# x, weights and result laid out by partitions, a finer fill of the head, turns in transposing mode and maxima through DRAM in a fused GFNet and gated feed-forward kernel

## The chip, the cores and the metric

The kernel runs on one core of a Trainium2 chip. The metric is the device time of that core in microseconds (us). Before the change the median of three runs is 418.23 us (418.14 to 418.61).

The engines are called by the profile's names: PE (TensorE, matrix products), PEld (loading of its weights), DVE (VectorE), ACT (ScalarE), POOL (GpSimd) and SP (SyncE, which here issues DMAs).

## The reference, cut to what matters

x has 2048 rows of 512 values; F is 1376.

```python
xn = _layernorm(x)                                   # over the last axis
s = irfft2(rfft2(xn, axes=(-2, -1)) * (w_r + 1j * w_i), s=(S, D), axes=(-2, -1))
gate, up = xn @ W_gate, xn @ W_up                    # 512 -> 1376
h = relu(gate) * up
return x + s * silu(h @ W_down)                      # 1376 -> 512
```

## The kernel before

Everything that PE multiplies is split into two numbers of 16 bits, a high and a low part, and each product is made in three passes (high by high, high by low, low by high). Scales keep the parts in range: for each block of 128 columns of the weights a power of two from the sum of their squares, for the down weights and for the Fourier filter one from a maximum over the whole matrix.

The 2048 rows of x are worked on in eight chunks of 256. A chunk is two "rows" of 128 partitions. The rows of x go over the partitions so that the first stage of the Fourier transform is a product with a 64 x 64 matrix. Feed-forward works on pairs of chunks, four blocks of 512 columns (the text calls them chunks 0 to 3 of the feed-forward, as the tiles' names do: `gu0_...` to `gu3_...`).

**The head.** x of chunks 0 and 1 and the gate and up weights (groups 0 to 6 of `GROUPS`, line 22; groups 0, 1 and 2 have one block of 128 columns, the others two) are loaded. `stats` (310) makes means and variances on DVE, `deviation` (321) their inverse roots (with a root `q` on ACT), `normalise` (365) `xf`. `turn_row` (399) turns one row of 128 by four products in 32 bits with a unit matrix from the constants `cS`; ACT copies the high part from PSUM into `xT`, DVE subtracts the low one. For the weights, ACT squares each block with a sum over the row (`squares`, 489, an `ACTIVATE` with two results, `wgu` and `m`, and a read of the accumulator), PE adds the partitions by a product with ones (`group_scale`, 499), DVE makes the scale `p`, then a high part `wgu<-raw,p` is made on ACT where `HIGH_ACT` says so (else on DVE) and a low part on DVE (`group_split`, 507). Twelve times three products of ones that nobody reads (`keep_busy`, 391, tile `idle`) run on PE first. The first three gate and up pairs are made in two halves of 256 columns (`product`, from 1033), all later ones on 512.

**The rest.** `product` makes a gate or up block `gu` of twelve products of 512 columns; ACT rectifies the gate block (`r`), DVE multiplies (`h32`), and high and low parts `h16` are made. `down` makes a group of three products `dn`. Between these PE runs the Fourier transform: eight first stages `s1` (`first_stage`, 24 products on 64 x 64 pieces each), whose split results `t1` go to DRAM (`A_d`); eight middle chunks (`fft_chunk`: `at` is loaded from `A_d`; on PE `y`, `xx`, `z` and `v`; between them DVE makes `a16`, `xsp`, the products `tt` with the filter, `pf`, `p16`, `z16` and `t9`), which store to `C_d`; eight last stages `s2` (`last_stage`, PE again in 64 x 64 pieces); and `finish` (976), which multiplies by the gate, adds x and stores. The down weights' maximum (`down_scale`) and the filter's (`filter_scale`) are made by `greatest` (551): a product that turns a column into a row, a maximum on DVE, and a product of ones that spreads it.

**What sets the order.** Nothing of this is issued in the order of the code. Each operation is a `step` (100) with an engine, a cost in us, what it reads and writes and perhaps a due time. `run` (119) works due times back through the dependencies and simulates the engines: at each point, of the steps of an engine that could begin within 0.06 us of the earliest, it takes the one that is due first. The order that comes out is the program's order on each engine, and each engine keeps it. Steps with a `mode` are products in small pieces (1 for the Fourier stages `s1`, `s2`, 2 for `y`, 3 for the last up product); the planner charges `MODE` us when PE changes between modes (182). The due times of the stages come from the table in lines 33 to 41 (`FIRST` and `FIRST_STEP` for the first stages, `MID` for the middle, `LAST` for the last ones, `DOWN` for the down weights), `tick` (668) gives those of the feed-forward. On chip, semaphores order what depends on each other. Most records of the profile have line 64, since the helper `InOrder` (56) issues every instruction; what an instruction is must be read from its tiles.

Of the kernel before, what the change touches and what calls it, by code (L numbers as in the profile page):

```python
# [230 lines left out]
def kernel(ctx: ExitStack, tc: tile.TileContext, x, wg, wu, wd, wl, ew, sp, c_r, c_d, c_m, c_x, c_s, out):  # L231
    nc = tc.nc
    PS = bass.MemoryType.PSUM
    xr, outr = (t[0].rearrange("(p e n) d -> e p n d", p=N1, n=NE) for t in (x, out))
# [33 lines left out]
    DVE.memset(ones, 1.0)  # L268
    warm = cpool.tile([P, 1], F32, name="warm")
# [22 lines left out]
    def load_x(c):  # L292
        tile_of(f"x{c}", "k4", [P, 2, D], F32)
        for e in range(2):
            engine, queue = (("SP", SP), ("ACT", ACT))[c == 0 and e]
            for i in range(2) if c == 0 else [None]:
                rows = slice(2 * c, 2 * c + 2) if i is None else slice(i, i + 1)
                to = slice(0, 2) if i is None else slice(i, i + 1)
                step(engine, .6, lambda e=e, queue=queue, rows=rows, to=to: queue.dma_start(T[f"x{c}"][64 * e:64 * e + 64, to], xr[e, :, rows, :]),
                     writes=[(f"x{c}", e, i)], lead=14 if c else None, kb=256 if i is None else 128, lag=2.2, due=(LOADX[c] + (i or 0) * .01) if c < 2 else None)  # L300
# [302 lines left out]
    def filter_scale(due):  # L603
# [323 lines left out]
    def last_stage(c, due):  # L927
# [24 lines left out]
        def put(e, op, to, a, b, n, reads, write, port=True):  # L952
            eng, cost = ((DVE, dve(n)), (POOL, pool(n)))[e == "POOL"]
# [228 lines left out]
```

## Time and profile before

| | before |
| --- | --- |
| runs, median | 418.23 us |
| the profiled execution | 417.77 us |
| its span | 416.0 us |
| PE busy | 404.9 us (97%) |
| DVE busy | 307.2 us (74%) |
| ACT busy | 188.4 us (45%) |
| POOL busy | 45.7 us (11%) |

The profile is one execution. Its span goes from the first to the last record, its own time is some 1.8 us longer. Times in the rows are from the span's start. An engine at 97% over the span can still be idle where it matters: the span's first 16 us and its last 5 are read apart from the rest. A row of the timeline gives start, length, engine, line, operation, what it writes `<-` what it reads, the shape and in brackets the idle time ahead of it and what ended that; a run of like instructions is one row with a count.

### The profile page before, as it was taken

How to read it: one execution, taken by the hardware profiler on the slowest of the kernel's cores; microseconds unless marked ns; L12 is line 12 of the kernel's file. 1: busy time of each engine (PE TensorE's matmuls, PEld its weight loads, DVE VectorE, ACT ScalarE, POOL GpSimd, SP SyncE). 2: the span in 40 equal slices, each digit the busy share in tenths (PEclk: the TensorE clock that was granted, in tenths of full speed). 3: DMA queues.
4: the chain of work that ended last, by engine and by line, in shares of the span. 5: the costliest groups of instructions: out<-in, count | busy, mean ns of one | idle time of the engine just before them, and what ended most of it. 6: DMA issues, size and time to landing. Idle time of an engine off the chain costs nothing.

```text
span 416.0 us, 7674 instructions
## 1 busy us (share of the span) xinstructions
PE 404.9 (97%) x2997; PEld 214.8 (52%) x2997; DVE 307.2 (74%) x648; ACT 188.4 (45%) x356; POOL 45.7 (11%) x68
## 2 busy tenths in 40 slices
PE   7799999999999999999999999999999999899995
PEld 5686454544444444545555456456455445444554
DVE  3748999999998898335585977897763427899943
ACT  3769863545444259420344335435414336432311
POOL 0000000000000000001130321330330018301300
PEclk9699999999999999999999999999999999999999
DMA  8992211055424787963005145053402189575614
GB/s 204 337 337 60 67 36 50 2 151 55 98 52 100 163 249 221 246 222 116 0 2 166 28 138 165 3 165 84 135 2 52 50 205 212 143 203 137 166 54 101
DMA packets 41764, 51.72 MB, mean 124 GB/s; under 512 B 16064, under 2 KB 24864, under 8 KB 41728
## 3 DMA queue, kind: packets, MB, share of 16 engines
q1 hardware_dynamic: 40880, 50.59, 45.6%
q10 hardware_dynamic: 848, 0.66, 0.6%
q8 instruction: 23, 0.38, 0.4%
q14 instruction: 13, 0.11, 0.1%
HBM read 35.48 MB, written 12.60 MB: 116 GB/s over the span
## 4 chain that ended last, share of the span: by engine, by line
PE 91%; DMA 5%; DVE 1%; ACT 1%; issue 0%; ACTq 0%; SPq 0%; DVEq 0%
PE gu L64 51%; PE dn L64 27%; PE z L64 3%; PE xx L64 3%; PE s L64 2%; DMA xt<-in_x 2%; DMA ct<-C_d 2%; PE y L64 2%; PE v L64 2%; DMA raw<-in_wu 1%; PE head L64 1%; PE dn_3b L64 1%; DVE xT L64 0%; DVE ye L64 0%; ACT xT L64 0%
## 5 line engine op out<-in xcount | busy, mean ns | idle before, releaser
L64 PE MATMUL gu<-xT,wgu 128*128 128x512 f16 (+1 forms) x1032 | 216.0, 367 | 3.4 <-ACT r L64 1.2
L64 PEld LDWEIGHTS <-wgu 128*128 128x128 f16 x1032 | 100.6, 99 | 108.4 <-issue 6.7
L64 PE MATMUL dn<-wds,h 128*128 128x512 f16 (+2 forms) x528 | 115.5, 372 | 0.0
L64 PEld LDWEIGHTS <-h 128*128 128x128 f16 (+1 forms) x561 | 53.7, 98 | 58.3 <-issue 2.5
L64 ACT ACTIVATE h<-h 128x512 f16<-128x512 f32 (+1 forms) x44 | 27.7, 629 | 70.2 <-DVE h L64 70.1
L64 DVE TENSOR_TENSOR h<-gu,r 128x512 f32<-128x512 f32 (+2 forms) x52 | 33.6, 646 | 22.6 <-PE gu L64 21.4
L64 POOL TENSOR_TENSOR po<-tt,tt 128x256 f32<-128x256 f32 x16 | 14.8, 926 | 285.1 <-DVE tt L64 236.8
L64 ACT ACTIVATE r<-gu 128x512 f32<-128x512 f32 (+1 forms) x44 | 26.0, 592 | 20.6 <-PE gu L64 20.3
L64 DVE TENSOR_TENSOR h<-h,h 128x512 f16<-128x512 f32 (+1 forms) x44 | 30.0, 690 | 4.5 <-ACT h L64 4.2
L64 POOL TENSOR_TENSOR ae<-zz 128x128 f32<-128x128 f32 (+1 forms) x32 | 19.3, 636 | 60.9 <-ACT zz L64 47.6
L64 DVE SCALAR_TENSOR_TENSOR tt<-xsp,cw,wt 128x512 f32<-128x512 f32 x32 | 25.2, 849 | 0.0
L64 ACT ACTIVATE g<-dn,cdi 128x512 f32<-128x512 f32 (+1 forms) x16 | 10.6, 673 | 25.1 <-PE dn L64 25.1
L64 DVE TENSOR_TENSOR z<-z,z 128x1024 f16<-128x1024 f32 x8 | 9.8, 1222 | 15.4 <-ACT z L64 15.4
L64 DVE TENSOR_TENSOR sv<-sv,g 128x512 f32<-128x512 f32 (+1 forms) x17 | 10.8, 671 | 9.6 <-ACT g L64 8.9
L64 DVE BATCH_NORM_STATS2 st<-x 128x6 f32<-128x512 f32 x16 | 10.9, 683 | 9.3 <-DMA x<-in_x 9.3
L64 PE MATMUL gu<-xT,wgt 128*64 128x256 f16 (+1 forms) x144 | 17.0, 309 | 0.0
L64 DVE TENSOR_TENSOR a<-y,a 128x1024 f16<-128x1024 f32 x8 | 9.7, 1218 | 8.3 <-ACT a L64 8.3
L64 ACT ACTIVATE wgu<-raw 128x512 f16<-128x512 f32 x20 | 12.4, 622 | 6.5 <-DMA raw<-in_wu 6.4
L64 DVE SCALAR_TENSOR_TENSOR wgu<-raw,p,wgu 128x512 f16<-128x512 f32 x20 | 14.5, 746 | 0.5 <-ACT wgu L64 0.4
L64 DVE TENSOR_TENSOR xt<-xt,sv 128x512 f32<-128x512 f32 (+1 forms) x17 | 11.5, 693 | 4.1 <-DMA xt<-in_x 4.1
L64 ACT ACTIVATE xs<-xs 128x1024 f16<-128x1024 f32 x8 | 8.5, 1058 | 12.6 <-DVE xs L64 12.6
L64 PEld LDWEIGHTS <-wgt 128*64 128x64 f16 (+1 forms) x144 | 9.6, 106 | 7.1 <-issue 1.7
(135 smaller groups left out, 432.5 us busy)
## 6 DMA issues: line engine op xcount, KB each, us to landing
A_d<-t SPq DMA_DIRECT2D x16, 256.0 KB, 3.2
rw<-in_wl SPq DMA_DIRECT2D x8, 512.0 KB, 6.5
wt<-in_wl SPq DMA_DIRECT2D x8, 512.0 KB, 4.7
at<-A_d SPq DMA_DIRECT2D x8, 512.0 KB, 4.6
C_d<-t SPq DMA_DIRECT2D x16, 256.0 KB, 3.3
ct<-C_d SPq DMA_DIRECT2D x16, 256.0 KB, 6.1
xt<-in_x SPq DMA_DIRECT2D x32, 128.0 KB, 3.0
out<-xt SPq DMA_DIRECT2D x30, 128.0 KB, 2.3
```

What stands on the lines that cost most here:

```text
L64: return lambda *args, **kw: self.tc.keep_in_program_order(f(*args, **kw))
```

## The change

1. **Layouts.** x, the result and the gate and up weights are put in DRAM by the host so that each partition's data lie together (for the weights group by group). A load of x is one DMA over 128 partitions in place of two over 64, a load of weights has one piece per partition in place of four, `finish` loads and stores once over 128 partitions. No load stands on ACT's queue any more: all are on SP's.
2. **The fill.** `keep_busy` issues 67 single products of ones in place of 36 in triples, as steps without due times, which the planner puts wherever PE would be waiting. They go to the upper half of a tile `small`, whose lower half takes the sums of the first two groups (so both have no `sum` tiles of their own).
3. **The turns.** The first chunks' rows are turned with PE's transposing operation; the unit matrix is made on POOL, and `cS` shrinks from 135 columns to 7.
4. **The maxima.** `greatest` stores the column to DRAM, loads it back spread over all partitions as rows, and reduces on DVE. The two products are gone.
5. **Joining.** Where PE has just run a step with a mode, the planner looks for steps with mode 1 or 2 that could begin and are due within `JOIN` (18.81 us) and prefers the same mode.
6. **Tables.** New due times; for the chunks 0 and 1 the first row of `xf` is made on ACT; other high parts on ACT; copies and sums of the last stage get a margin of 0.4 us in the plan.

```diff
-T0, DOWN, FIRST, FIRST_STEP, MID, MID_STEP, LAST, LAST_STEP = 10.0, 56.9, 49.0, 16.8, 180.6, 14.5, 265.2, 14.8
+T0, DOWN, FIRST, FIRST_STEP, MID, MID_STEP, LAST, LAST_STEP = 7.1, 57.9, 51.9, 17.1, 155.2, 14.9, 307.4, 10.8
...
-NORM, TURN1 = (('DVE', 'DVE'), ('DVE', 'ACT')), 'PE'
+NORM, TURN1 = (('ACT', 'DVE'), ('ACT', 'DVE')), 'PE'
...
-                    t, s = min((k for k in at if k[0] <= soon), key=lambda k: (k[1].due, k[1].order))
+                    now = [k for k in at if k[0] <= soon]
+                    if e == "PE" and mode:
+                        now = [k for k in now if 0 < k[1].mode < 3 and k[1].due < k[0] + JOIN] or now
+                    t, s = min(now, key=lambda k: (e == "PE" and k[1].mode != mode if mode else 0, k[1].due, k[1].order))
...
+    POOL.memset(unit, 0.0)
+    POOL.affine_select(out=unit, in_=unit, compare_op=ALU.not_equal, fill=1.0, base=0, pattern=[[-1, P]], channel_multiplier=1)
...
+        for i in range(1 + (c == 0)):
+            rows = slice(i, i + 1) if c == 0 else slice(0, 2)
+            step("SP", .5, lambda rows=rows: SP.dma_start(T[f"x{c}"][:, rows], x[:, 2 * c + rows.start:2 * c + rows.stop, :]),
...
-            step("PE", .43, lambda: [matmul(T["idle"], w[:, 0:P], w, start=True, stop=True) for _ in range(3)],
-                 writes=["idle"], due=1. + .43 * k, lead=0.)
+            step("PE", .213 if k < 26 else .11, lambda: matmul(T["small"][:, 256:], w[:, 0:P], w, start=True, stop=True), writes=[("small", "idle")])
...
-                matmul(head()[:, cols], T[f"xf{c}"][:, i, cols], cS[:, 7:], start=True, stop=True)
-        step("PE", 1., run, reads=[(f"xf{c}", i), "cS"], writes=[(f"head{c}", i)])
+                PE.transpose(head()[:, cols], T[f"xf{c}"][:, i, cols], unit)
+        step("PE", .45, run, reads=[(f"xf{c}", i)], writes=[(f"head{c}", i)])
...
-        step("PE", .31, lambda: matmul(T[f"row_{name}"][0:1, :], col, cS[:, 7:], start=True, stop=True),
-             reads=["cS", *reads], writes=[f"row_{name}"], due=due, margin=MARGIN)
-        step("DVE", .25, lambda: DVE.tensor_reduce(top[0:1, :], T[f"row_{name}"][0:1, :], axis=AX.X, op=ALU.max),
-             reads=[f"row_{name}"], writes=[f"max_{name}"])
-        step("PE", .31, lambda: matmul(T[f"all_{name}"], ones[0:1, :], top[0:1, :], start=True, stop=True),
-             reads=[f"max_{name}"], writes=[f"all_{name}"], due=due + 2, margin=MARGIN)
+        step("SP", .6, lambda: SP.dma_start(row.rearrange("a p -> p a"), col), reads=reads, writes=[f"row_{name}"], due=due, kb=8)
+        step("SP", .6, lambda: SP.dma_start(rows, row.broadcast_to([P, P])), reads=[f"row_{name}"], writes=[f"rows_{name}"], kb=64)
+        step("DVE", .22, lambda: DVE.tensor_reduce(top, rows, axis=AX.X, op=ALU.max), reads=[f"rows_{name}"], writes=[f"all_{name}"], due=due + 6)
...
+            step("SP", .5, lambda t=t, cols=cols: SP.dma_start(out[:, 2 * c + i, cols], t()), reads=[(n, part)], kb=w // 2, due=due, lag=2.2)
```

What the planner makes of it on the engines, at the places that the prediction speaks of. First ACT in the head, before (`wgu,m<-raw` is a square with its sum, `wgu<-raw,p` a high part, `xT<-head` the copy of a turned row; the digit behind `wgu` and `raw` is the group):

```order
L64 DMA x0_115<-in_x 64x512 x2
L64 DMA raw0_1_126<-in_wu 128x4x128
L64 ACTIVATE wgu0_76,m0_173<-raw0_1_126 128x512
L64 ACTIVATE q0_171<-q0_171 128x2
L64 ACTIVATE wgu0_76,m0_173<-raw0_0_131 128x512
L64 ACTIVATE wgu1_77,m1_186<-raw1_0_139 128x512
L64 ACTIVATE wgu1_77,m1_186<-raw1_1_144 128x512
L64 ACTIVATE wgu0_76<-raw0_0_131,p0_201 128x512
L64 ACTIVATE xT0_214<-head0_196 128x512 x2
L64 ACTIVATE wgu0_76<-raw0_1_126,p0_201 128x512
```

And ACT at the same place with the change:

```order
L64 ACTIVATE q0_172<-q0_172 128x2
L64 ACTIVATE wgu0_77,m0_193<-raw0_0_133 128x512
L64 ACTIVATE xf0_196<-x0_121,q0_172 128x512
L64 ACTIVATE wgu0_77,m0_193<-raw0_1_137 128x512
L64 ACTIVATE xT0_222<-head0_208 128x512 x2
L64 ACTIVATE wgu1_78,m1_240<-raw1_0_141 128x512
L64 ACTIVATE wgu0_77<-raw0_0_133,p0_233 128x512
L64 ACTIVATE wgu1_78,m1_240<-raw1_1_146 128x512
L64 ACTIVATE wgu2_79,m2_260<-raw2_0_154 128x512
L64 ACTIVATE wgu2_79,m2_260<-raw2_1_158 128x512
```

ACT's two kinds of DMA issue are gone, a row of `xf` is new on it, and the two `xT` copies stand behind three rows in place of five squares and high parts. Behind the rows shown come the root for chunk 1, two high parts of group 1, three squares of group 3, a high part of group 2, chunk 1's row of `xf`, one more square and the two `xT` copies of chunk 1. On PE the order is now 44 products of the fill, four transposes (the row of `xf` from DVE), two of the fill, four transposes (the row from ACT), two of the fill, the sum of group 0, 19 of the fill, the sum of group 1 and the first product; before it was 36 of the fill, the sum of group 0, eight products with the unit matrix, the sum of group 1 and the first product. SP's queue begins with x of chunk 0 (two DMAs), x of chunk 1 and then the weights group by group; before it began with `cS`, half of x of chunk 0, weights, and x of chunk 1 only behind group 1.

Then SP's queue where the Fourier transform's middle begins, before (`t1` to `A_d` is the store of a first stage, `at` the load for a middle chunk, `DMA_TRANSPOSE` a turn of x for the feed-forward's last chunk):

```order
L64 DMA_TRANSPOSE xT3_1866<-x16_6_1652 128x16x128
L64 DMA_TRANSPOSE xT3_1866<-x16_7_1671 128x16x128
L64 DMA cX_74<-in_c_x 64x256
L64 DMA cD_73<-in_c_d 128x2048
L64 DMA cm0_1971<-in_c_m 128x512
L64 DMA A_d_69<-t1_7_1965 128x1x1024 x2
L64 DMA wt_0_1988<-in_wl 128x1024
L64 DMA at_0_2027<-A_d_69 128x2x1024
L64 DMA wt_0_1988<-E_d_71 2x2x128
L64 DMA at_1_2136<-A_d_69 128x2x1024
```

And with the change (`rows_mw` is the filter's maximum, loaded back):

```order
L64 DMA rows_mw_111<-row_mw_110 128x128
L64 DMA E_d_71<-edge2_114 64x2x16
L64 DMA wt_0_1791<-E_d_71 2x2x128
L64 DMA A_d_69<-t1_6_1892 128x1x1024 x2
L64 DMA A_d_69<-t1_7_1910 128x1x1024 x2
L64 DMA cm1_1957<-in_c_m 128x512
L64 DMA_TRANSPOSE xT3_1975<-x16_6_1690 128x16x128
L64 DMA at_0_1988<-A_d_69 128x2x1024
L64 DMA at_1_1992<-A_d_69 128x2x1024
```

One turn now stands between the last store to `A_d` and the first load from it, the other behind both loads. Before, both stood ahead of the store.

Last, DVE where the middle's first chunks pass, before:

```order
L64 TENSOR_TENSOR z16_0_2408<-z0_2366,z16_0_2408 128x1024
L64 TENSOR_TENSOR xsp_1_2427<-xx1_2395,xo1_2425 128x256
L64 TENSOR_TENSOR xsp_1_2427<-xx1_2395,xo1_2425 128x4x32
L64 TENSOR_TENSOR xsp_1_2427<-xo1_2425,xx1_2395 128x4x32
L64 SCALAR_TENSOR_TENSOR tt0_1_2433<-xsp_1_2427,cw_87,wt_1_2194 128x512
L64 SCALAR_TENSOR_TENSOR tt1_1_2448<-xsp_1_2427,cw_87,wt_1_2194 128x512
L64 SCALAR_TENSOR_TENSOR tt2_1_2452<-xsp_1_2427,cw_87,wt_1_2194 128x512
L64 SCALAR_TENSOR_TENSOR tt3_1_2454<-xsp_1_2427,cw_87,wt_1_2194 128x512
L64 TENSOR_TENSOR h32_2_1_2475<-gu2_1_1_2435,r2_1_2450 128x512
L64 TENSOR_TENSOR pf_1_2526<-po_1_2456 128x4x32 x4
L64 TENSOR_TENSOR t9_0_2528<-v0_2458,t9_0_2528 128x2x512
L64 TENSOR_TENSOR a16_2_2547<-y2_2477,a16_2_2547 128x2x8x64
```

And with the change:

```order
L64 TENSOR_TENSOR a16_2_2404<-y2_2346,a16_2_2404 128x2x8x64
L64 TENSOR_TENSOR pf_1_2328<-po_1_2308 128x4x32 x4
L64 TENSOR_TENSOR p16_1_2451<-pf_1_2328,p16_1_2451 128x1024
L64 TENSOR_TENSOR z16_0_2459<-z0_2426,z16_0_2459 128x1024
L64 TENSOR_TENSOR xsp_2_2481<-xx2_2462,xo2_2479 128x256
L64 TENSOR_TENSOR xsp_2_2481<-xx2_2462,xo2_2479 128x4x32
L64 TENSOR_TENSOR xsp_2_2481<-xo2_2479,xx2_2462 128x4x32
L64 SCALAR_TENSOR_TENSOR tt0_2_2514<-xsp_2_2481,cw_88,wt_2_2254 128x512
L64 SCALAR_TENSOR_TENSOR tt1_2_2516<-xsp_2_2481,cw_88,wt_2_2254 128x512
L64 SCALAR_TENSOR_TENSOR tt2_2_2536<-xsp_2_2481,cw_88,wt_2_2254 128x512
L64 SCALAR_TENSOR_TENSOR tt3_2_2541<-xsp_2_2481,cw_88,wt_2_2254 128x512
L64 TENSOR_TENSOR z16_1_2534<-z1_2489,z16_1_2534 128x1024
```

Chunk 1's filter products are now made before `z16` of chunk 0, and those of chunk 2 come between `z16` of chunk 0 and that of chunk 1; with them the chunks stand closer together. The middle begins ahead of the last up product of the feed-forward's chunk 1 and its down groups; before it began behind that product and the down groups of two of the four rows.

The joining shows on PE. Before, two pairs of the sixteen `s` stages stood together (`s2` of chunks 1 and 2, and of 3 and 4). Now seven do: `s1` of chunks 0 and 1, 4 and 5, 6 and 7, and `s2` of 0 and 1, 2 and 3, 4 and 5, 6 and 7; `y` of chunks 0 and 1 is one block too. Runs of products in small pieces, each entered from large products, are 23 in place of 27. The last pair of `s2` now stands behind the last up product of the feed-forward's chunk 3; before, `s2` of chunk 7 stood just ahead of it.

More of the change, by code (lines that the diff above doesn't have):

```diff
@@ L293, in load_x @@
         tile_of(f"x{c}", "k4", [P, 2, D], F32)
[L294 to L300, printed above, removed]
+        for i in range(1 + (c == 0)):
+            rows = slice(i, i + 1) if c == 0 else slice(0, 2)
+            step("SP", .5, lambda rows=rows: SP.dma_start(T[f"x{c}"][:, rows], x[:, 2 * c + rows.start:2 * c + rows.stop, :]),
+                 writes=[(f"x{c}", i)], lead=14 if c else None, kb=256 * (rows.stop - rows.start), lag=2.2, due=(LOADX[c] + i * .01) if c < 2 else None)
     def x_names(c, i):
-        return [(f"x{c}", e, None if c else i) for e in range(2)]
+        return [(f"x{c}", 0 if c else i)]
     def stats(c, q, j):
@@ L481, in load_group @@
         w = sum(fwidth(f) for f in GROUPS[g])
-        f0 = GROUPS[g][0] * P
         for i, src in enumerate((wg, wu)):
-            tile_of(f"raw{g}_{i}", "k4", [P, 4, 2 * P], F32)
-            e, queue = (("SP", SP), ("ACT", ACT))[g == 0 and i]
-            step(e, .6, lambda i=i, src=src, queue=queue: queue.dma_start(T[f"raw{g}_{i}"][:, :, :w], src.rearrange("(k p) f -> p k f", p=P)[:, :, f0:f0 + w]),
+            tile_of(f"raw{g}_{i}", "k4", [P, 4, w], F32)
+            of = src[:, 4 * P * GROUPS[g][0]:4 * (P * GROUPS[g][0] + w)].rearrange("p (k f) -> p k f", k=4)
+            step("SP", .5, lambda i=i, of=of: SP.dma_start(T[f"raw{g}_{i}"], of),
                  writes=[f"raw{g}_{i}"], lead=12 if g else None, kb=2 * w, lag=2.5, due=LOADS[g])
@@ L500, in group_scale @@
         nf = len(GROUPS[g])
-        tile_of(f"sum{g}", "dn" if g < 2 else "F", [P, 4], F32)
+        if g > 1:
+            tile_of(f"sum{g}", "F", [P, 4], F32)
+        to, name = ((lambda: T[f"sum{g}"]), f"sum{g}") if g > 1 else ((lambda: T["small"][:, 4 * g:4 * g + 4]), ("small", g))
         tile_of(f"p{g}", "p", [P, 2, 4], F32)
-        step("PE", .2, lambda: matmul(T[f"sum{g}"][:, :2 * nf], ones, T[f"m{g}"][:, :2 * nf], start=True, stop=True),
-             reads=[(f"m{g}", j, i) for j in range(nf) for i in range(2)], writes=[f"sum{g}"])
-        step("DVE", .52, lambda: scale_of(T[f"sum{g}"][:, :2 * nf], T[f"p{g}"][:, :, :2 * nf], 9), reads=[f"sum{g}"], writes=[f"p{g}"], port=True)
+        step("PE", .2, lambda: matmul(to()[:, :2 * nf], ones, T[f"m{g}"][:, :2 * nf], start=True, stop=True),
+             reads=[(f"m{g}", j, i) for j in range(nf) for i in range(2)], writes=[name])
+        step("DVE", .52, lambda: scale_of(to()[:, :2 * nf], T[f"p{g}"][:, :, :2 * nf], 9), reads=[name], writes=[f"p{g}"], port=True)
     def group_split(g):
@@ L585, in run @@
             b = p.bitcast(I32)
-            DVE.tensor_scalar(p[:, 0:1], T["all_md"], 1e-30, 1e30, op0=ALU.max, op1=ALU.min)
+            DVE.tensor_scalar(p[:, 0:1], all_md, 1e-30, 1e30, op0=ALU.max, op1=ALU.min)
             DVE.tensor_scalar(b[:, 0:1], b[:, 0:1], 0x7F800000, None, op0=ALU.bitwise_and)
@@ L952, in put @@
         def put(e, op, to, a, b, n, reads, write, port=True):
-            eng, cost = ((DVE, dve(n)), (POOL, pool(n)))[e == "POOL"]
-            step(e, cost, lambda: getattr(eng, op)(to(), a(), b()), reads=reads, writes=[write], port=port)
+            eng, cost = ((DVE, dve(n)), (POOL, pool(n) + .2))[e == "POOL"]
+            step(e, cost, lambda: getattr(eng, op)(to(), a(), b()), reads=reads, writes=[write], port=port, margin=LATE)
         def copy(to, of, reads, write):
-            step("ACT", .11, lambda: ACT.activation(to(), of(), AF.Copy), reads=reads, writes=[write])
+            step("ACT", .11, lambda: ACT.activation(to(), of(), AF.Copy), reads=reads, writes=[write], margin=LATE)
         copy(lambda: ac()[:, :, 64:65], lambda: a0()[:, :, 64:65], [zn], (aen, 4))
@@ L986, in finish @@
             step("DVE", dve(w), lambda s=s, t=t: DVE.tensor_add(t(), t(), s()), port=True,
-                 reads=[(sn, 3 + i, part), (n, "x", 0), (n, "x", 1)], writes=[(n, part)])
-            for e in range(2):
-                engine, queue = (("SP", SP), ("ACT", ACT))[e and c == NCH - 1 and i]
-                step(engine, .6, lambda t=t, cols=cols, e=e, queue=queue: queue.dma_start(outr[e, :, 2 * c + i, cols], t()[64 * e:64 * e + 64]),
-                     reads=[(n, part)], kb=w // 4, due=due, lag=2.2)
+                 reads=[(sn, 3 + i, part), (n, "x")], writes=[(n, part)])
+            step("SP", .5, lambda t=t, cols=cols: SP.dma_start(out[:, 2 * c + i, cols], t()), reads=[(n, part)], kb=w // 2, due=due, lag=2.2)
     step("SP", .6, lambda: SP.dma_start(cR, c_r), writes=["cR"], lead=20, kb=256)
-    step("SP", .6, lambda: SP.dma_start(cS, c_s), writes=["cS"], kb=70, due=LOADU)
+    step("SP", .6, lambda: SP.dma_start(cS, c_s), writes=["cS"], kb=4, lead=20)
     step("SP", .6, lambda: SP.dma_start(cD, c_d), writes=["cD"], lead=20, kb=512)
     step("SP", .6, lambda: SP.dma_start(cX, c_x), writes=["cX"], lead=20, kb=128)
+    tile_of("small", "dn", [P, D], F32)
     keep_busy(BUSY)
@@ L1180 @@
     r = run_bass_kernel_spmd(nc, [arrays], core_ids=[0])
-    return r.results[0]["out_0"]
+    return np.asarray(r.results[0]["out_0"]).reshape(2, N1, NE, D).transpose(1, 0, 2, 3).reshape(1, S, D)
```

45 lines of the change are left out of this document (23 added, 22 removed).

## The prediction, made before the changed kernel ran

> **What bounds the kernel now.** I read the page's chain first, then the waits of TensorE (PE), then the head stage by stage. The page says how much of the span PE works, and which work ended last:
>
> ```profile
> PE 404.9 (97%) x2997; PEld 214.8 (52%) x2997; DVE 307.2 (74%) x648; ACT 188.4 (45%) x356; POOL 45.7 (11%) x68
> PE 91%; DMA 5%; DVE 1%; ACT 1%; issue 0%; ACTq 0%; SPq 0%; DVEq 0%
> ```
>
> The answer on who waited for whom has few rows for PE, here the two longest (us in total, times, longest):
>
> ```profile
> PE sum L64 <- ACT wgu L64: 1.5, 1, 1.5
> PE gu L64 <- ACT r L64: 1.2, 1, 1.2
> ```
>
> The first lies in the head, ahead of the first product, as do the shorter ones left out; the second is far behind. So the time is that of PE's own stream, plus what comes before the first product, plus the tail. A change pays in three ways only: the products start earlier, PE's stream gets shorter, or a wait of PE goes. The head cut into windows (PE's busy us and count, then PEld, DVE, ACT, POOL, PE clock, DMA share, GB/s):
>
> ```profile
> 0.00:3.45 3.45, 2.40 (x12) 1.71 (x13) 0.19 (x2) 1.49 (x2) 0.20 (x4) 1.00 0.34 95
> 3.45:6.87 3.42, 3.42 (x18) 2.42 (x17) 0.97 (x3) 0.00 (x0) 0.00 (x0) 1.00 0.97 245
> 6.87:10.28 3.41, 1.50 (x13) 1.06 (x11) 2.26 (x9) 2.14 (x7) 0.00 (x0) 0.99 1.12 271
> 10.28:13.70 3.42, 3.42 (x16) 3.42 (x17) 1.46 (x5) 1.35 (x4) 0.00 (x0) 0.51 1.15 266
> 13.70:17.11 3.41, 1.30 (x12) 0.98 (x12) 2.93 (x9) 3.16 (x8) 0.00 (x0) 0.99 1.08 359
> 17.11:20.52 3.41, 3.41 (x19) 2.43 (x17) 3.27 (x12) 3.13 (x9) 0.00 (x0) 0.51 1.05 381
> ```
>
> A window in which PE was busy for 1.50 or 1.30 us is followed by one at half clock (0.51). The second of these holds products: it costs 1.7 us.
>
> **The head.** These rows carry it, in order of time (start, duration):
>
> ```profile
> 4.58 0.69 DVE L64 BATCH_NORM_STATS2 st<-x 128x6 f32<-128x512 f32 x1 [3.56 <-DMA x<-in_x]
> 6.78 0.69 DVE L64 BATCH_NORM_STATS2 st<-x 128x6 f32<-128x512 f32 x1 [1.28 <-DMA x<-in_x]
> ...
> 8.74 0.61 ACT L64 ACTIVATE wgu<-raw 128x512 f16<-128x512 f32 x1
> 9.26 0.19 ACT L64 ACTIVATION_READ_ACCUMULATOR wgu<-raw 128x1 f32 x1
> ...
> 10.25 3.66 PE L64 MATMUL head<-cS,xf 128*128 128x128 f32 x16 [0.37 <-DVE xf L64]
> ...
> 16.40 5.65 PE L64 MATMUL gu<-xT,wgu 128*128 128x256 f16 x35 [1.05 <-DVE xT L64]
> ...
> 23.34 1.95 PE L64 MATMUL head<-cS,xf 128*128 128x128 f32 x16
> 25.12 8.22 PE L64 MATMUL gu<-xT,wgu 128*128 128x256 f16 x72
> ```
>
> Products run from 16.40; at 25.12 plus 24 of them (8.22/72 = 0.114 each), so at 27.8, the first three gate and up pairs are done for half the rows. From there PE's only wait is the 1.2 for r. I ask when the changed kernel gets to that point.
>
> Its loads stand on one queue: x of chunks 0 and 1 (1.05 MB), then the first weights (0.26 MB). By the windows' rates 1.17 MB have moved by 6.87 and the rest at 271 GB/s by 7.4; x, now alone in front, lands near 4.2 and 4.8 instead of 4.58 and 6.78 (estimate: the first DMA leaves 0.4 earlier and shares with nothing). So the statistics end near 6.1, and **ScalarE (ACT) becomes the pace setter**. Its durations, by form:
>
> ```profile
> L64 ACT ACTIVATE wgu<-raw,p 128x512 f16<-128x512 f32 x11 | 7.6, 716 | 0.2
> L64 ACT ACTIVATE xT<-head 128x512 f16<-128x512 f32 x4 | 2.3, 596 | 5.1 <-PE head L64 5.0
> L64 ACT ACTIVATE xf<-x,q 128x512 f32<-128x512 f32 x1 | 0.8, 816 | 0.1
> ```
>
> A square with its read takes 0.71 (8.74 to 9.45). In the new order from 7.4: square 8.1, xf 8.9, square 9.6, two xT 10.8, square 11.5, high part 12.3, square 13.0; PE's sum for the second group stands ahead of the first product, so that starts near 13.2 (16.40 before). Behind it: two squares, q (0.2), two high parts, three squares, a high part, xf: 19.7. PE's four products (12 x 0.114 = 1.4 each) are done by 18.8, so it waits 0.9 for these rows of x. The eight transposes have no row. With the old form sixteen passes take 25.12 - 23.34 = 1.8; sixteen at half a 256-column product are 0.9, eight 0.5; below that nothing, since they must stream. I take 0.6, nearest the eight. Then two products: 23.0. **Gain 4.8.** If only PE's work bound it (18.8 + 0.6 + 2.7 = 22.1), 5.7; with one half-clock window left among the products, 3.1. The early copies that this needs are covered by DVE's and ACT's idle time; without that cover the gain falls to the 3.2 of the earlier start alone.
>
> The fill: 44 unread products stand ahead of the first transpose. As before, 30 of them (12 + 18 in the first two windows) run by 6.87, and the other 14, at 0.114, last to about 8.5; the first row of xf is ready at 7.9, the second at 8.9. So the fill costs the first transposes 0.6, which the 13.2 does not feel: ACT's two squares and the high part end later than its xT copies anyway. The identity made on GpSimd (POOL) has no row; it has 7 us to be ready, beside nothing on that engine. I take nothing, at most 1.
>
> **The maxima.** Where a product of one row breaks into the stream:
>
> ```profile
> 36.08 18.29 PE L64 MATMUL gu<-xT,wgu 128*128 128x512 f16 x84
> 54.21 0.28 PE L64 MATMUL sum<-m,ones 128*128 128x4 f32 x2
> ...
> 60.52 5.35 PE L64 MATMUL gu<-xT,wgu 128*128 128x512 f16 x24
> 65.81 0.38 PE L64 MATMUL row_md<-cS,md 128*1 128x128 f32 x2
> 66.12 2.76 PE L64 MATMUL gu<-xT,wgu 128*128 128x512 f16 x12
> ```
>
> 84 products take 18.13, 0.216 each. So 24 from 60.52 end at 65.70, and the next begins at 66.12: 0.42, four times: **1.7 gained**. In their place come two DMAs, one behind the other, for each maximum. A like round trip is that of A_d:
>
> ```profile
> 169.25 0.85 PE L64 MATMUL s<-xs,cR 64*64 64x257 f16 x24
> ...
> 173.09 1.19 SPq L64 DMA_DIRECT2D A_d<-t  x2
> ...
> 178.25 0.39 SPq L64 DMA_DIRECT2D at<-A_d  x1
> ...
> 182.34 0.20 DVE L64 COPY am<-at 128x126 f16<-128x126 f16 x1 [3.04 <-DMA at<-A_d]
> ```
>
> From the store's issue to the loaded data that is 9.2 for 0.5 MB each way; 8 KB and 64 KB should take less, and not less than half: 4.6 to 9.2, I take 6. On SP the loads of x for chunks 2 and 3 queue behind it; DVE reads them thirteen rows after the reduction that waits for the same trip, so I cost that at nothing. On VectorE (DVE) the reduction stands twelve rows behind md's (five of 0.75, two of 0.69, smaller ones, about 6 in sum), so DVE stands still for 0 to 3. PE has four products of 2.6, two first stages and five more before the first down product, 21 in all, against about 15 until the first weights are split (their low part stands behind t of stage 0 on DVE, which is later than the trip). Cost 0.
>
> **Joined stages.** Single and paired last stages before:
>
> ```profile
> 339.40 0.85 PE L64 MATMUL s<-ct,cR 64*64 64x257 f16 x24
> 340.19 2.76 PE L64 MATMUL gu<-xT,wgu 128*128 128x512 f16 x12
> 342.88 1.51 PE L64 MATMUL s<-ct,cR 64*64 64x257 f16 x48
> 344.33 2.76 PE L64 MATMUL gu<-xT,wgu 128*128 128x512 f16 x12
> 347.02 1.51 PE L64 MATMUL s<-ct,cR 64*64 64x257 f16 x48
> 348.47 5.35 PE L64 MATMUL gu<-xT,wgu 128*128 128x512 f16 x24
> ```
>
> Twelve products take 2.59, so the entry at 342.88 costs 0.10; a stage alone takes 0.79 + 0.10, a pair 1.45 + 0.10: 0.23 for each pair. The order has 7 pairs of s against 2, and y of chunks 0 and 1 in one: 6 x 0.23, less 2 lost neighbourhoods of unlike stages at 0.1: **1.2 gained**. The wait of 1.2 for r came behind five stages within 9.1 us (339.40 to 348.47), all of which ACT copies out; now they come in twos with four products between: **1.2 gained** (0 if another takes its place).
>
> **The FFT's middle** starts earlier in PE's row, ahead of chunk 1's last up product and its down groups. Before, its first data came 13.1 after the last forward stage (169.25 to 182.34). Now the order gives PE 17 us of work from stage 6 to the first y (the pair, five products, four down groups of 0.65). The data needs 13.1, 0.7 for the second stage, and on SP a transposing DMA now stands ahead of the load of at (min, median, max ns):
>
> ```profile
> L64 SPq DMA_TRANSPOSE xT<-x x6: 1738/2766/6637, 99.1 to 168.9; - x6
> ```
>
> If its issue (1.7 to 6.6, median 2.8) fell wholly behind the store, y could begin after 15.5 to 20.4, 16.6 by the median: ready by about the time PE comes. A little later DVE is the tighter one:
>
> ```profile
> L64 DVE SCALAR_TENSOR_TENSOR tt<-xsp,cw,wt 128x512 f32<-128x512 f32 x32 | 25.2, 849 | 0.0
> L64 DVE TENSOR_TENSOR z<-z,z 128x1024 f16<-128x1024 f32 x8 | 9.8, 1222 | 15.4 <-ACT z L64 15.4
> ```
>
> From the start of z_1 on PE to v_1 there are z_1 (1.3), v_0 (0.8), and five down groups of 0.65: 5.4. DVE has z_0 (1.2), three xsp (1.0), four tt (3.4), z_1 (1.2): 6.8, some 0.5 less where they overlap: v_1 waits about 0.9. **I take 1.2 lost** in this stretch, 0 to 4 as bounds.
>
> **The tail** after the last product (411.2) is one chain of copy, two DVE rows and a store. It stays, with one store of 128 partitions for two of 64:
>
> ```profile
> 408.43 2.79 PE L64 MATMUL dn_3b<-wds,h 128*128 128x256 f16 x24
> ```
>
> I take 0.1 lost. Halved issues on SP and the last stage's new margins touch no engine that PE waits for; nothing.
>
> **Sum**, against the profiled execution's 417.77 (span 416.0; the median of the runs is 418.23, 0.1% more): 4.8 + 1.7 + 1.2 + 1.2 - 1.2 - 0.1 = 7.6, so **410.2**.
>
> **Rivals.** *More from the head, nothing lost later*: ACT's squares arrive in better rhythm, PE's work alone binds (5.7), the middle loses nothing: 408.1. For it: DMA ran at 359 to 381 later in the head. *The clock still falls*, the change doing less than it says: the fill stops before xf, and the transposes leave a window as thin as 1.50; one half-clock window among the products costs 1.7: 411.9. For it: only 0.2 of fill stands between the transposes. The trace shows nothing of transposing mode. The Trainium skill, "TensorE: Matmul & The Clock Gate", Part 4, says that full clock "doesn't engage for transpose-mode (it doesn't count as PE-busy the same way)", which would favour this rival; no run here shows it yet, and by it the time would be 411.9. *The middle eats the gain*: at 4 lost there and a new wait for r, 414.2. *Slower*: the same mechanism in full. Every chunk's z and v wait for DVE, which is at 74% and gets its eight chunks closer together; 16 such waits pass the 8.8 gained elsewhere from 0.55 each on, and at 0.7 each the time is 420.2. Against it: of those sums only v_1's came out short.
>
> **How the numbers follow.** Forecast 410.2, chance 0.52; more head 0.15; clock 0.11; middle 0.13; slower 0.05; the rest (0.04) unchanged, gains and losses cancelling. The lower bound is all gains at their best, 417.77 - 5.7 - 1.7 - 1.4 - 1.2 = 407.8, less 0.8 for loads that land earlier: 407. The upper takes the small head (3.1) and 3.4 lost in the middle with the r wait kept: 417.77 - 3.1 - 1.7 - 1.2 + 3.4 = 415.2. A measurement of this kernel tells about 0.2% from no change.
>
> **What would show it.** First product near 13.2, the third pair's end near 23.0; granted clock 0.99 in every window from 6.87; no row_ or all_ product; gaps of 0.10 at four fewer entries; no wait of PE for r; a wait before v_1 of about 1. Wrong it would be by a clock of 0.5 after the transposes, by PE waits for DVE spread over the middle, or by a late identity.

## The result and the profile after: 1.5% slower

The changed kernel's median is 423.77 us (423.28 to 424.98), against 418.19 for the kernel before: a ratio of 1.0148, with a 95% interval of 1.0108 to 1.0188. The prediction was 410.2 in a range of 407.0 to 415.2. It was wrong, and in the sign.

First the page of the changed kernel, its engines' busy time and the chain that ended last:

```profile
span 422.3 us, 7638 instructions
PE 404.0 (96%) x3004; PEld 215.0 (51%) x3004; DVE 300.1 (71%) x648; ACT 187.1 (44%) x357; POOL 44.6 (11%) x70
PE 64%; DVE 19%; DMA 11%; ACT 3%; issue 1%; SPq 1%; DVEq 0%
PE gu L64 33%; PE dn L64 18%; DVE h L64 3%; PE z L64 3%; PE xx L64 2%; DVE xs L64 2%; DVE t L64 2%; DMA xT<-x 2%; DMA row_md<-md 2%; PE small L64 2%; PE y L64 2%; DMA row_mw<-mw 2%; PE s L64 2%; PE v L64 2%; DVE wds L64 2%; DVE wgu L64 1%
```

PE held 91% of the chain before and holds 64% now. Two stores of half a kilobyte (`row_md`, `row_mw`) have 2% each, as much as all of `xx`. That is the first hint.

Next the head, windows as before (PE, PEld, DVE, ACT, POOL, PE clock, DMA share, GB/s), and then PE's rows:

```profile
6.87:10.28 3.41, 3.41 (x34) 3.05 (x33) 2.10 (x6) 2.33 (x6) 0.00 (x0) 1.00 1.05 398
10.28:13.70 3.42, 3.01 (x27) 2.33 (x25) 2.91 (x9) 3.42 (x10) 0.00 (x0) 1.00 1.03 420
13.70:17.11 3.41, 3.41 (x34) 3.08 (x33) 3.03 (x11) 3.41 (x11) 0.00 (x0) 1.00 1.04 399
```

```profile
13.21 1.47 PE L64 MATMUL gu<-xT,wgu 128*128 128x256 f16 x12
...
18.65 1.09 PE L64 MATMUL head<-unit,xf 128*128 128x128 f32 x8
19.58 8.02 PE L64 MATMUL gu<-xT,wgu 128*128 128x256 f16 x72
```

The clock is full in all of them. The first product begins at 13.21, and the third pair's first half ends at 19.58 + 24 x 8.02/72 = 22.25, against 27.86 before: the head gained 5.6. So all of the loss, and more, lies behind. PE's waits there (engine waited for; us, times, longest):

```profile
PE gu L64 <- ACT r L64: 3.7, 1, 3.7
PE gu L64 <- DVE h L64: 3.0, 3, 1.3
PE y L64 <- DMA at<-A_d: 2.3, 1, 2.3
PE dn L64 <- DVE h L64: 2.2, 1, 2.2
PE dn L64 <- ACT r L64: 1.6, 1, 1.6
```

That is 12.8 in place of 1.2. Two windows behind such waits are at half clock (0.51, the third figure from the end; the first stands behind the 1.6 and the 2.2, the second behind the 2.3 for `at`):

```profile
78.54:81.95 3.41, 3.41 (x10) 1.19 (x9) 3.35 (x7) 1.71 (x3) 0.00 (x0) 0.51 0.01 2
180.93:184.34 3.41, 3.25 (x105) 3.10 (x105) 1.49 (x3) 2.08 (x3) 0.00 (x0) 0.51 1.18 288
```

Half of 3.41 twice is another 3.4 (an estimate). What stood still ahead of these places is told by SP's rows and DVE's (start, duration, in brackets the idle time and what ended it):

```profile
55.55 0.33 SPq L64 DMA_DIRECT2D row_md<-md  x1
64.50 0.32 SPq L64 DMA_DIRECT2D rows_md<-row_md  x1
64.91 0.86 SPq L64 DMA_DIRECT2D x<-in_x  x2
...
152.44 0.33 SPq L64 DMA_DIRECT2D row_mw<-mw  x1
...
160.64 0.33 SPq L64 DMA_DIRECT2D rows_mw<-row_mw  x1
```

```profile
69.77 0.29 DVE L64 TENSOR_REDUCE max_md<-rows_md 128x1 f32<-128x128 f32 x1 [8.98 <-DMA rows_md<-row_md]
...
165.53 0.29 DVE L64 TENSOR_REDUCE max_mw<-rows_mw 128x1 f32<-128x128 f32 x1 [6.56 <-DMA rows_mw<-row_mw]
```

The reader is to see three things. The store of one column takes at most 8.9 us, from its issue at 55.55 to the issue of the load that waits for it at 64.50, and the load 5.3 more: 14.2 for the trip, 13.1 for the second (152.44 to 165.53). DVE stands still for 9.0 and 6.6 of it. And SP's queue stands too: the two loads of x wait behind `rows_md` until 64.91.

### The profile page after: what moved, and what is told of

Same layout as the page of the kernel before. It is cut to its first block, busy times and chain, and to the rows that moved or that the text cites. A ratio compares the mean times of both kernels' runs of the same rounds, so it can differ in the third digit from the quotient of the medians.

```text
span 422.3 us, 7638 instructions
## 1 busy us (share of the span) xinstructions
PE 404.0 (96%) x3004; PEld 215.0 (51%) x3004; DVE 300.1 (71%) x648; ACT 187.1 (44%) x357; POOL 44.6 (11%) x70
## 4 chain that ended last, share of the span: by engine, by line
PE 64%; DVE 19%; DMA 11%; ACT 3%; issue 1%; SPq 1%; DVEq 0%
PE gu L64 33%; PE dn L64 18%; DVE h L64 3%; PE z L64 3%; PE xx L64 2%; DVE xs L64 2%; DVE t L64 2%; DMA xT<-x 2%; DMA row_md<-md 2%; PE small L64 2%; PE y L64 2%; DMA row_mw<-mw 2%; PE s L64 2%; PE v L64 2%; DVE wds L64 2%; DVE wgu L64 1%
## 5 line engine op out<-in xcount | busy, mean ns | idle before, releaser
L64 PE MATMUL gu<-xT,wgu 128*128 128x512 f16 (+1 forms) x1032 | 213.8, 364 | 6.7 <-ACT r L64 3.7
L64 PE MATMUL dn<-wds,h 128*128 128x512 f16 (+2 forms) x528 | 117.6, 376 | 3.8 <-DVE h L64 2.2
L64 POOL TENSOR_TENSOR ae<-zz 128x128 f32<-128x128 f32 (+1 forms) x32 | 17.1, 571 | 79.3 <-ACT zz L64 70.9
L64 DVE TENSOR_TENSOR sv<-sv,g 128x512 f32<-128x512 f32 (+1 forms) x17 | 10.8, 672 | 7.9 <-ACT g L64 7.4
L64 ACT ACTIVATE t<-s 128x896 f16<-128x896 f32 (+1 forms) x16 | 8.5, 595 | 15.2 <-DVE t L64 7.7
L64 DVE SCALAR_TENSOR_TENSOR wgu<-raw,p,wgu 128x512 f16<-128x512 f32 x20 | 14.4, 747 | 0.6 <-ACT wgu L64 0.6
L64 ACT ACTIVATE t<-v 128x1024 f16<-128x1024 f32 x8 | 8.2, 1022 | 13.8 <-PE v L64 13.6
L64 DVE BATCH_NORM_STATS2 st<-x 128x6 f32<-128x512 f32 x16 | 10.8, 676 | 4.6 <-DMA x<-in_x 4.6
L64 ACT ACTIVATE wds<-wds,scd 128x512 f16<-128x512 f32 (+1 forms) x11 | 7.9, 721 | 13.7 <-DVE scd L64 7.7
L64 DVE TENSOR_TENSOR t<-v,t 128x1024 f16<-128x1024 f32 x8 | 9.7, 1218 | 4.9 <-ACT t L64 4.9
```

Of the source, the lines that this page charges most:

```text
L64: return lambda *args, **kw: self.tc.keep_in_program_order(f(*args, **kw))
```

## The experiments

Medians are of three rounds. The kernel before ran beside each group with medians of 416.7 to 418.2, so ratios to it carry across groups, microseconds only within about 1.

| run | us | ratio to before | 95% interval |
| --- | --- | --- | --- |
| the change | 423.8 | 1.0148 | 1.0108 to 1.0188 |
| no_wait_both | 417.0 | 0.9994 | 0.9972 to 1.0015 |
| no_wait_md | 419.7 | 1.0055 | 1.0022 to 1.0087 |
| no_wait_mw | 421.3 | 1.0101 | 1.0085 to 1.0116 |
| maxima_on_pe | 409.8 | 0.9825 | 0.9811 to 0.9840 |
| no_trip | 408.8 | 0.9788 | 0.9753 to 0.9822 |
| trip_on_pool | 421.3 | 1.0089 | 1.0061 to 1.0117 |
| trip_on_pool_no_wait | 409.5 | 0.9805 | 0.9773 to 0.9837 |
| trip_lag_told | 408.5 | 0.9795 | 0.9751 to 0.9839 |
| wide_store | 413.2 | 0.9921 | 0.9892 to 0.9949 |
| fill_of_36 | 412.2 | 0.9883 | 0.9857 to 0.9909 |
| fill_of_transposes | 408.6 | 0.9803 | 0.9776 to 0.9829 |
| turns_by_matmul | 410.3 | 0.9838 | 0.9811 to 0.9864 |
| trips_in_before | 430.5 | 1.0318 | 1.0284 to 1.0353 |
| wide_store_told | 413.6 | 0.9918 | 0.9891 to 0.9945 |

### Is it the wait for the trips?

The edit, for both names, for `md` alone and for `mw` alone:

```diff
+        of = rows
+        if name in ('md', 'mw'):
+            of = cpool.tile([P, P], F32, name=f"fixed_{name}")
+            DVE.memset(of, 1e4)
-        step("DVE", .22, lambda: DVE.tensor_reduce(top, rows, axis=AX.X, op=ALU.max), reads=...
+        step("DVE", .22, lambda: DVE.tensor_reduce(top, of, axis=AX.X, op=ALU.max), reads=...
```

> The changed kernel, in which DVE's two reductions of greatest read a constant tile: the DMAs run as before and nobody waits for them, so the down weights and the filter get a fixed scale. The order of the work on every engine is that of the changed kernel. Theory (the two trips through DRAM stop DVE, and with it PE): the changed kernel lost PE waits of 1.6 + 2.2 behind the first trip and 3.7 + 0.5 + 2.3 behind the second, and two half-clock windows of 1.7 behind them, 13.7 in all, so 423.8 - 13.7 = 410; if the two waits of 1.3 for h at 123 and 154 come from the first trip as well, 407.6. Rival (the new order itself is too tight, the trips only mark the places): most of these waits stay, 417 or more.

> As the run without both waits, but only the first reduction (the down weights' maximum) reads a constant tile. Theory: 1.6 + 2.2 + 1.7 = 5.5 go, 418.3, or 415.7 with the two waits of 1.3 for h. Rival: at most 2 of the 5.5 go, the rest comes back as a wait for h behind, 421.5 or more.

> As the run without both waits, but only the second reduction (the filter's maximum) reads a constant tile. Theory: 3.7 + 0.5 + 2.3 + 1.7 = 8.2 go, 415.6. Rival (PE would wait for the load of at anyway, since the middle stands too early in the order): the 2.3 and its half-clock window stay, 419.6 or more.

> The changed kernel with the maxima on PE as before (with the unit matrix in place of the constants' one); all other parts of the change stay. The planner makes some of the order anew (508 of PE's 5960 rows differ). Theory: as without both waits, plus four products that break in at 0.42 each: 411.9 (409.3 if the waits for h at 123 and 154 go too). Rival (the rest of the change is at fault): 417 or more.

`greatest` of the kernel before, on the new `unit`, gave 409.8: all of the loss is the trips', and the rest of the change is worth 7 us. That bore the theory out. But the three runs without DVE's waits missed it: they gave back 6.8, 4.0 and 2.5 us instead of 13.7, 5.5 and 8.2. no_wait_both came out at the rival's edge (417.0), no_wait_mw within the rival's range, and there the wait of PE for `at` stayed, with 1.9, as the rival said. Whether the order itself is too tight, as the rival has it, is not settled by maxima_on_pe, whose order differs in part; the next group keeps the order. What else waits shows in DVE's waits of no_wait_both between 50 and 186:

```profile
DVE am L64 <- DMA at<-A_d: 5.4, 1, 5.4
DVE st L64 <- DMA x<-in_x: 4.0, 2, 2.7
DVE wt L64 <- DMA wt<-E_d: 3.8, 1, 3.8
```

DVE waits here for three other DMAs that stand on SP's queue behind the loads of the trips. Two of the waits go with the trips: no_trip, below, has 0.8 for x and none for `wt`. The longest does not, since no_trip has 5.7 for `at` without any trip. In maxima_on_pe the two loads of x were issued at 37.35 and 39.01; here SP held them until 65.79. A second cost was to be tested: the queue.

### DVE's wait and SP's queue apart

no_trip keeps the order of the changed kernel with the four DMAs left out, and both reductions read the constant tile. In the other two POOL issues the DMAs, and in the last of them the reductions read the constant tile too:

```diff
-        step("SP", .6, lambda: SP.dma_start(row.rearrange("a p -> p a"), col), ...
-        step("SP", .6, lambda: SP.dma_start(rows, row.broadcast_to([P, P])), ...
+        step("SP", .6, lambda: POOL.dma_start(row.rearrange("a p -> p a"), col), ...
+        step("SP", .6, lambda: POOL.dma_start(rows, row.broadcast_to([P, P])), ...
```

> The changed kernel's order with the four DMAs of greatest left out, and both reductions on a constant tile (fixed scales). The run in which only DVE's waits were taken away came to 416.95, 7 below the changed kernel and 7 above the one with maxima on PE. Theory (a trip costs twice: DVE waits for it, and the SP queue stands still behind its store and its load, so that loads of x, the stores to A_d and the load of at are late): with both gone 408, the 409.8 of the maxima on PE less four breaks of 0.42. Rival (the new order of the middle is too tight by itself): 414 or more.

> The changed kernel with the four DMAs of greatest issued by POOL, which has no other DMA; DVE still waits for them. Theory: SP's queue no longer stands still, worth about the 8 between the runs without DVE's waits (417) and without trips (408): 416 to 418. Rival (the queue matters only where DVE doesn't wait anyway): 422 to 424.

> As the trips on POOL, and both reductions read a constant tile: the DMAs run and nobody waits for them, on DVE or on SP. Theory: as with no trip at all, 408 (within 1). Rival (the DMAs themselves disturb, by traffic or by their writes): 411 or more.

| | SP's queue stands | SP's queue is free |
| --- | --- | --- |
| DVE waits | 423.8 | 421.3 |
| DVE does not wait | 417.0 | 409.5 (408.8 with no DMA at all) |

Without either cost the order of the changed kernel runs at 409, so that order is not too tight. DMAs that nobody waits for cost at most the 0.7 between 409.5 and 408.8, which the intervals do not tell from nothing; 409.5 is a little above the 409 that was expected at most. DVE's wait alone costs 421.3 - 409.5 = 11.8, the queue alone 417.0 - 408.8 = 8.2 (7.5 against 409.5), both 15.0. They overlap: the sum of the two is larger than what both cost together. So trip_on_pool missed its expectation (416 to 418) and came near its rival's (422 to 424): freeing the queue helps little as long as DVE stands. Its PE waits:

```profile
PE gu L64 <- ACT r L64: 3.7, 1, 3.7
PE dn L64 <- DVE h L64: 2.2, 1, 2.2
PE gu L64 <- DVE h L64: 1.9, 2, 1.2
PE y L64 <- DMA at<-A_d: 1.6, 2, 1.1
```

Neither r nor h has to do with the maxima. They are work that stands behind the waiting reductions in DVE's order (the row that follows the first reduction at 69.77 makes h, at 69.97), and ACT's work behind DVE's.

### The trip told to the planner, and the trip made short

```diff
-        ... writes=[f"row_{name}"], due=due, kb=8)
+        ... writes=[f"row_{name}"], due=due, kb=8, lag=8.3)
-        ... writes=[f"rows_{name}"], kb=64)
+        ... writes=[f"rows_{name}"], kb=64, lag=4.7)
```

> The changed kernel with the planner told what the trips took here: 8.3 us behind the store and 4.7 behind the load in place of 2.2 each. It then puts the reductions later in DVE's order and moves much else (1852 of PE's 5960 rows differ). Theory (the order was made with trips half as long): most of DVE's 9.0 and 6.6 are filled, SP's stand remains: 411 to 417. Rival (nothing can fill them, PE needs the down weights and the filter by then): 421 or more.

408.5, better than the 411 to 417 expected: the trips are still there and no shorter (the second takes 15.8, from 140.74 to 156.53), and the kernel is 2% faster than the one before the change. All that PE waits for in this run, by the same view:

```profile
PE small L64 <- DVE md L64: 1.1, 1, 1.1
PE head L64 <- ACT xf L64: 0.4, 1, 0.4
PE small L64 <- DVE p L64: 0.2, 1, 0.2
PE small L64 <- ACT wgu L64: 0.2, 1, 0.2
```

All four rows lie in the head. Told the length, the planner put other work of DVE ahead of the first reduction, and it begins with no wait; the second waits 1.4.

> The changed kernel, but greatest stores all columns (12 of md, 11 of mw) instead of one, so that each of the 128 partitions writes 48 or 44 bytes next to each other in place of 4, and loads all of them back (768 and 704 KB in place of 64); the order is that of the changed kernel. In the changed kernel the stores took 8.9 and 8.1 us to land, the loads 5.3 and 4.9. Theory (it is the 4-byte pieces side by side that make the store slow: other stores of 8 to 256 KB took 2.6 to 3.3): the stores land in about 3.5, the loads take about 6, DVE waits some 4 less each time: 418 to 421. Rival (a store of pieces this small takes 8 to 9 whatever their size): stores as before, loads and reductions longer, 424 to 427.

The edit gives `greatest` all columns (`md` and `mw` whole) and makes `row` and `rows` as many times wider. SP's rows at the first trip:

```profile
56.02 0.33 SPq L64 DMA_DIRECT2D row_md<-md  x1
57.67 0.32 SPq L64 DMA_DIRECT2D rows_md<-row_md  x1
58.05 0.90 SPq L64 DMA_DIRECT2D x<-in_x  x2
```

and the reduction on DVE:

```profile
62.34 1.75 DVE L64 TENSOR_REDUCE max_md<-rows_md 128x1 f32<-128x1536 f32 x1 [1.12 <-DMA rows_md<-row_md]
```

A store of 48 bytes from each of 128 partitions landed within 1.65 us, one of 4 bytes in 8.9. The load of 768 KB took 4.6. DVE waits 1.1 in place of 9.0, and the time falls to 413.2, below what theory and rival said. Left behind the head are PE waits of 2.3 for `at` and 1.9 for h, and some slow clock behind the first.

> The changed kernel with the wide store (48 and 44 bytes for each partition) and the planner told its times: 1.1 us behind the store, 4 behind the load, 1.7 for the reduction. Theory (what was left of the loss with the wide store, 413.2, was order made for another reduction): no wait for r, h or at behind the trips, 408 to 409.5, no better than the told long trips (408.5), since PE has no wait left there. Rival (the wide load of 768 KB and the longer reductions cost in this order too): 411 or more.

413.6, a miss: the waits for h and r are gone, but the planner's new order has this on SP's queue, and this PE wait:

```profile
162.48 3.04 SPq L64 DMA_DIRECT2D A_d<-t  x4
165.62 0.77 SPq L64 DMA_DIRECT2D wt<-in_wl  x1
166.48 6.71 SPq L64 DMA_TRANSPOSE xT<-x  x2
173.43 0.92 SPq L64 DMA_DIRECT2D at<-A_d  x2
```

```profile
PE y L64 <- DMA at<-A_d: 3.8, 1, 3.8
```

Two transposing DMAs, 6.7 us together, now stand between the last store to `A_d` and the load of `at`; the changed kernel has one there, of 3.5, and trip_lag_told one of 1.6. So the planner underrates this step too (2 us each in the code), and telling it the trip's time bought nothing here. How much of the 408.5 of trip_lag_told is luck of its order was not tried.

### The trips in the old kernel

> The kernel before with the trips of greatest through DRAM as in the changed kernel, and nothing else of the change (old tables, old head, the planner's lag of 2.2). The planner makes part of the order anew (1012 of PE's rows). Theory (the planner puts the reduction where a short trip would end, so DVE and SP stand still here too): 2 to 4 PE waits and one or two half-clock windows, less four breaks of 0.42: 421 to 428. Rival (the loss needs the changed kernel's tighter order): 415 to 418.

The kernel before, with only `greatest` of the change: 430.5, above the range expected (421 to 428), 13.7 slower than without. The trips took 15.0 and 14.4 us here. So the loss does not need the new order. The largest wait, on PE, is for the scale that stands behind the second trip:

```profile
194.00 4.68 PE L64 MATMUL dn<-wds,h 96*128 96x512 f16 x13 [5.85 <-DVE pw L64]
```

### The head

All three on the order of trip_lag_told, 408.5. First the fill:

```diff
-BUSY, LATE, PAIR1, PAIR2 = 67, 0.4, 0, 0
+BUSY, LATE, PAIR1, PAIR2 = 36, 0.4, 0, 0
```

> The kernel in which the planner was told the trips' real length (408.5), with 36 unread products in the fill in place of 67; the order on all other engines stays. Theory (a window with little PE work is followed by one at half clock, as in the kernel before): PE's fill ends near 6.5, the windows 6.87 to 10.28 and 10.28 to 13.70 are thin, and the windows behind them, 10.28 to 17.11, show a clock near 0.5; products from 13.2 on are slowed for up to 3.4 us, so the third pair ends 1.7 later, and the time is 409.5 to 410.3. Rival (the sums and transposes keep the clock up, the fill is of no use): 0.99 in all windows, 408.5.

Windows of that run:

```profile
6.87:10.28 3.41, 2.25 (x19) 1.70 (x17) 2.07 (x6) 2.04 (x5) 0.00 (x0) 1.00 1.02 383
10.28:13.70 3.42, 0.76 (x6) 0.66 (x7) 2.77 (x7) 3.39 (x9) 0.00 (x0) 1.00 1.03 404
13.70:17.11 3.41, 3.41 (x19) 2.51 (x18) 3.01 (x11) 3.41 (x12) 0.00 (x0) 0.51 1.05 391
17.11:20.52 3.41, 3.41 (x33) 3.06 (x31) 3.12 (x11) 2.42 (x6) 0.00 (x0) 0.99 1.05 404
```

A window with 0.76 of PE work is followed by one at 0.51, as expected; the window of 2.25 is followed by one at 1.00, against the expectation. The third pair ends 1.8 later. The time is 3.7 higher; the other 1.9 came behind (a PE wait of 1.1 for a turned x among it) and were not expected.

Then the fill made of transposes:

```diff
-... lambda: matmul(T["small"][:, 256:], w[:, 0:P], w, start=True, stop=True), ...
+... lambda: PE.transpose(T["small"][:, 256:256 + P], ones, unit), ...
```

> The kernel in which the planner was told the trips' real length (408.5), with each of the 67 unread products of the fill replaced by one transposing of ones, 128 x 128 in 32 bits; the order of all else stays. Theory (transposes in 32 bits count as work of PE): they run at 0.117 each as the eight of chunk 1 did, the clock is 1.00 from the second window on, 408.5. Rival: the fill doesn't raise the clock, it is near 0.5 up to 13.7 or 17.1, products start at half speed, 409.5 to 411. The rival's rule is that of the Trainium skill, "TensorE: Matmul & The Clock Gate", Part 4: full clock doesn't engage for transpose mode.

```profile
3.45:6.87 3.42, 3.42 (x25) 3.42 (x24) 2.60 (x9) 0.20 (x1) 0.00 (x0) 1.00 0.87 258
6.87:10.28 3.41, 2.24 (x21) 2.00 (x20) 2.43 (x7) 1.69 (x4) 0.00 (x0) 1.00 1.01 362
10.28:13.70 3.42, 3.13 (x27) 2.66 (x25) 2.15 (x6) 3.29 (x10) 0.00 (x0) 1.00 1.03 414
13.70:17.11 3.41, 3.38 (x32) 3.08 (x33) 3.14 (x9) 3.41 (x10) 0.00 (x0) 1.00 1.04 387
```

With no other work than transposes of 32 bits up to 10.8 the clock is 1.00 throughout, and the time is the same (408.6). The figure of the clock does not show the start, where PE is slower although it reads 1.00: the first transposes stand some 0.2 apart (9 in 2.18 us from 1.36), later ones 0.12 (12 in 1.47 from 5.57). The products of the fill in trip_lag_told get faster at about the same place (11 in 2.53 from 1.05, 12 in 1.54 from 5.51).

Last the turns by products with `unit`:

> The kernel in which the planner was told the trips' real length (408.5), with the sixteen turns of the head made by 32-bit products with the unit matrix, as before the change, in place of transposing; the order stays. Theory: sixteen took 1.8 before, eight transposes 0.9, so the four of the second row stand some 0.4 longer ahead of xT, the first product begins 0.3 to 0.5 later, and the eight of chunk 1 cost 0.9 more: third pair's end 1.0 to 1.4 later, 409.5 to 409.9. Rival (ACT sets the pace there anyway): the third pair ends within 0.5, 408.5 to 409.

```profile
19.45 2.05 PE L64 MATMUL head<-unit,xf 128*128 128x128 f32 x16
21.34 7.92 PE L64 MATMUL gu<-xT,wgu 128*128 128x256 f16 x71
```

Chunk 1's turns take 1.89 in place of the 0.93 (18.70 to 19.63) of trip_lag_told, the first product begins at 14.00 in place of 13.25, and the third pair ends 1.7 later. The time is 1.8 higher; both are somewhat above what was expected (1.0 to 1.4, and 409.9 at most). Of the head's gain of 5.6, 1.7 comes from the transposing operation.

## Why the prediction was wrong, step by step

**The failed step is the maxima**: "8 KB and 64 KB should take less, and not less than half: 4.6 to 9.2, I take 6", and "Cost 0". The trip took 14.2 and 13.1. The row taken as its nearest, the trip of `A_d`, moves 1024 elements of each partition, the store of a maximum one; bytes were compared, and that bound was none. The changed kernel's view of the DMAs (pieces, KB each, median us to landing) has the stores to `A_d` at

```profile
A_d<-t SPq DMA_DIRECT2D x16, 256.0 KB, 3.3
```

and the store of half a kilobyte took 8.9. The step from a trip's length to DVE's wait was sound, its cost of 0 not quite: in wide_store the first trip takes 6.3 (56.02 to 62.3) and DVE waits 1.1, within the 0 to 3 said, but the kernel is still 4.4 above no_trip (with the longer reductions and the second trip of 7.6). The second trip, for the filter, was given no reckoning of its own in the prediction; DVE stood 6.6 for it.

**The second half of the step failed as well**: the loads of x behind the trip were costed at nothing, since DVE reads them behind the same reduction. SP's standing queue alone costs 8.2 (417.0 against 408.8). With it DVE waits 3.2 longer for x and 3.8 for `wt`, and PE 2.4 longer for h and 1.5 for `at`, than in no_trip.

**The third** is that no rival named a longer trip. The rival for slower had DVE's share in the middle as its mechanism; DVE's busy time fell to 300.1, and PE waits for v in no run here. The time came out slower for another reason.

The other terms can be read from no_trip, which has the changed kernel's order without the trips (its span 407.2 against 416.0):

| term | forecast | measured |
| --- | --- | --- |
| head: third pair's end | 4.8 earlier | 5.7 (22.17 against 27.86) |
| from there to the last product: maxima off PE, joins, r wait, less the middle | 1.7 + 1.2 + 1.2 - 1.2 = 2.9 | 2.6 (380.8 against 383.4) |
| tail | -0.1 | 0.5 (4.2 against 4.8 from the last product to the span's end) |
| sum without trips | 7.6 | 8.8 |
| the two trips | 0 | 15.0 |

In the head the first product's 13.2 was met (13.21). The eight transposes took 0.93, at the bound given for sixteen, not the 0.6 taken; but PE did not wait for chunk 1's rows, so the end came 0.7 earlier than said. The clock held, the rival against it fell. The wait for r at 354 is gone, no v waits, and all that PE waits for behind the head in no_trip is 0.8 for h, ahead of the middle, and 0.4 for `at`. That makes the 1.2 at which the middle was put, but by luck: the forecast had it from a wait for v. How the 2.6 is shared between joins and maxima was not tried apart; maxima_on_pe, with the four breaks back and in part another order, is 1.0 above no_trip, where 1.7 was forecast. The fear about the transposing DMA ahead of `at` was right in kind: it is what wide_store_told loses by.

## What to carry to other kernels

Do not bound a small DMA's time by its bytes: here 6 KB landed in 1.65 us and 0.5 KB in 8.9. Take the time from a row with like pieces, or leave it open on the long side. In an order made by a planner, a wrong duration costs twice: the engine that was told to wait stands, and so does everything in order behind it, the DMA queue too. Try telling the planner the measured time before changing the design: here two numbers turned 1.5% slower into 2% faster. It is no sure gain, since wide_store_told (413.6 against 413.2) got nothing from it.

## What the runs showed of the hardware that was not expected

A store to DRAM of 4 bytes from each of 128 partitions, side by side, took 8 to 10.5 us in every run here, whether SP or POOL issued it (SP 8.2 to 10.5, POOL 7.9 to 8.6, up to the landing or to the issue of the load that waits for it); 48 and 44 bytes from each took at most 1.65 and 3.2. Whether the size of the piece counts or that many pieces share a small stretch of DRAM was not tried. The Trainium skill, "DMA: Bandwidth & Descriptors", Specifications, says that below 512 bytes a DMA reads, modifies and writes; both stores are far below it, so that line by itself does not tell the 8.9 from the 1.65.

Transposing in 32 bits keeps the clock at 1.00, and PE gets to full speed with nothing else on it (fill_of_transposes). The Trainium skill, "TensorE: Matmul & The Clock Gate", Part 4, states the opposite for transpose mode; for this form the run decides against it, and no run here has one in 16 bits.
